# Thresholded attention with a gated mix: the first batch's softmax division moved behind the attended values, and a third PSUM room for scores at the start

## The chip, the cores and the metric

One NeuronCore of a Trainium2 chip runs the whole program. The metric is the device time of one execution in microseconds (us); a run's time is that of its slowest core, and here there is one. A profiled execution has its own time and, a little shorter, its span: from the first to the last instruction that the profile shows.

## The reference

There are 8 batches of 8 heads, 576 positions and a head size of 64. Attention keeps only the scores within `tau` of their row's maximum; the attended values of a batch's heads, side by side, are the input of a gated mix with 512 channels.

```python
scores = scale * np.matmul(q, k.transpose(0, 1, 3, 2))
thresh = np.max(scores, axis=-1, keepdims=True) - tau
scores = np.where(scores >= thresh, scores, -1000000000.0)
scores = scores - np.max(scores, axis=-1, keepdims=True)
attn = np.exp(scores)
attn = attn / (np.sum(attn, axis=-1, keepdims=True) + 1e-09)
x = np.matmul(attn, v)                     # heads side by side: (batch, 576, 512)
...
for k in range(K):                         # K = 5
    gate_pre += conv_w[k][None, None, :] * xp[:, k:k + S, :]
gate = 1.0 / (1.0 + np.exp(-gate_pre))
val = x @ w_val
return (gate * val @ w_out).astype(np.float32)
```

## The kernel before

A **job** is two heads of one batch: 32 jobs, four for each batch. A job has two **halves** of the query positions (320 and 256 columns, `W`), and its scores come in nine **tiles** of 128 rows by 576 keys: four query blocks for each of the two heads, and one tile that holds the last 64 positions of both heads ("both"). A **group** is what is turned together: the two heads' tiles of one query block, side by side in a `pp` buffer, or the "both" tile in the `pl` buffer.

A tile passes through these steps (class `Tile`):

- `multiply` (L493, TensorE): the scores, into one of two PSUM rooms `s` of two banks each (`r_s`).
- `largest` (L497, VectorE): the row maximum, negated, into `nm`.
- `weigh` (L503 and L505, ScalarE): the exponential into `e`, and the threshold into `nm`.
- `keep` (L519, VectorE): scores over the threshold keep their weight, into `pp` or `pl`, and a column of `sums` takes the row sum. With it the room `s` becomes free.

Then the group's softmax division (`Group.turned`): 1e-9 is added on GpSimd (L536), VectorE makes the reciprocal (L538), and each tile's 576 columns are multiplied by it on GpSimd (L549) or ScalarE (L545), whichever the planner finds free. TensorE turns the divided weights in three steps of three 128x128 transposes (L599; the "both" tile: four and one) into one of two one-bank rooms `tp`, and ScalarE copies each step into `T` (L610, L615, L621). When a half's `T` is full, `attended` multiplies it with the values (L643) into a one-bank room `acc` and ScalarE copies that to `xT` (L651). These matmuls come in pairs, one for each head, and the two heads fill different halves of the array's columns. The first pair takes the last 64 keys and stands there as three pieces:

```python
pieces = [(0, NKC, 0, SL), (1, NKC, 0, w), (0, NKC, SL, w)]
```

The mix needs `xT`: in the first batch its five taps are float32 matmuls with diagonal matrices (L690, GpSimd makes the diagonals at L677), in the other batches they run on GpSimd and VectorE (L730, L737). The two 512x512 products (L784) of a batch fill gaps of TensorE while the next batches' tiles are worked on. Job 0's scores are float32 matmuls of the raw inputs; from job 1 on they are made of two parts each (`KH`, `KL`, `Q`), which ScalarE (L331, L340) and GpSimd (L292) split and SyncE's DMA queue lays out. In the first batch VectorE, ScalarE and GpSimd also unpack both weight matrices, in sixteen blocks (`Words`, `from_f64`).

The order of all instructions is written out by a planner in the kernel (`op`, `carry_out`): every operation has an engine, a cost, a due time, what it comes after, and the rooms it takes and gives. The planner walks through its own time and emits, on each engine, the ready operation that is due first. Engines then work off their instructions strictly in that order. PSUM has eight banks: four are the rooms `s`, two `tp`, two `acc`.

Of the kernel before, what the change touches and what calls it, by code (L numbers as in the profile page):

```python
# [10 lines left out]
F32 = mybir.dt.float32  # L11
# [7 lines left out]
P = 128  # L19
# [2 lines left out]
DIVIDE = ("ACT",)  # L22
DUE = (8, 8, 8)
PACE_M = 0.17
ON_PE = (0, 1, 2, 3)


@with_exitstack
def tile_thresholded_attention_gated_mix(
# [42 lines left out]
    ps_a = ctx.enter_context(tc.tile_pool(name="ps_a", bufs=1, space=bass.MemoryType.PSUM))  # L72

    ctx.enter_context(tc.manual_schedule())

# [119 lines left out]
    r_pp = Rooms(att, 3, [P, 2 * S], F32, "pp")  # L195
    r_pl = Rooms(att, 1, [P, S + SL], F32, "pl")
    r_sums = Rooms(att, 5, [P, 4], F32, "sums")
    r_T = Rooms(pt, 2, [P, 2 * NKC + 1, W[0]], F32, "T")
    r_xT = Rooms(mix, 2, [P, PAD + S], F32, "xT")
    r_xh = Rooms(mix, 6, [P, S], F32R, "xh")  # L200
# [231 lines left out]
            self.lent = lambda: room.rearrange("p (e s) -> p e s", e=NE)  # L432


    class Tile:
        def __init__(self, k, t, h, qc, grp):
            self.k, self.t, self.h, self.qc, self.grp = k, t, h, qc, grp
            i = h or 0
            both = h is None
            if both:  # L440
                after = t.blocks if t.i == 0 else [t.high_k, t.low_k, *t.blocks]
            elif t.i == 0:
                after = [t.first[h]]
            else:
                after = t.copied
            if tiles:
                after = after + [tiles[-1].scores]
# [12 lines left out]
            if TH == "ACT":  # L460
                after = [op("ACT", k - DUE[1], 0.83, 1.0, self.weigh, [largest], [r_e])]
            else:
                after = [
                    op("ACT", k - DUE[1], 0.64, 0.78, self.weigh, [largest], [r_e]),
                    op("DVE", k - 9, 0.13, 0.13, self.level, [largest]),
                ]
            room = [] if i else [r_pl if both else r_pp]
            if i:
                after.append(grp.kept)
            grp.kept = op(  # L470
                "DVE", k - DUE[2], 0.74, 0.96, self.keep, after, room + ([] if i else [r_sums]),
                [(r_s, lambda: self.s), (r_e, lambda: self.e), (r_nm, lambda: self.nm)],
            )

        def multiply(self):
            t, h, qc = self.t, self.h, self.qc
# [37 lines left out]
        def keep(self):  # L514
            grp, i = self.grp, self.h or 0
            if i == 0:
                grp.p = (r_pl if grp.both else r_pp).take()
                grp.sums = r_sums.take()
            nc.vector.scalar_tensor_tensor(  # L519
                grp.p[:, i * S : (i + 1) * S].rearrange("p (a f) -> p a f", a=2),  # L520
                self.s[:, :, :HS], self.nm[:, 1:2], self.e,
                op0=ALU.is_ge, op1=ALU.mult, accum_out=grp.sums[:, i : i + 1],
            )

    class Group:


        def __init__(self, half, off, both):
            self.half, self.off, self.both = half, off, both

        def turned(self, k):

            n = 1 if self.both else 2
            sums = lambda: self.sums[:, 0:n]
# [25 lines left out]
            if self.both:  # L560
                divided.append(op("POOL", k - 4, 0.21, 0.3, lambda: spread(
                    self.p[:, S : S + SL], self.p[:, S - SL : S]), divided))
            parts = [(0, NKC), (NKC, 1)] if self.both else [(0, 3), (3, 3), (6, 3)]
            out = []
            for c0, m in parts:
                last = c0 + m == (NKC + 1 if self.both else 2 * NKC + 1)
                half = self.half
                turn = op(
                    "PE", k - 3 + 0.1 * c0, 0.109 * m, 0.109 * (m - 1) + 0.35, self.turn(c0, m),
                    divided if last else divided[0 : 1 + c0 // 3 * (n - 1)], [r_tp],  # L570
                    [(r_pl if self.both else r_pp, lambda: self.p)] if last else [],
                )
# [53 lines left out]
    class Half:  # L626
        def __init__(self, t, j):
            self.t, self.j = t, j
            self.T, self.begun, self.room, self.copies = None, False, [], []

        def attended(self, k):
            t, j = self.t, self.j
# [2 lines left out]
            def attend():  # L635
                acc = self.acc = r_acc.take()
                T = self.T[:, :, 0:w]
                pieces = [(0, NKC, 0, SL), (1, NKC, 0, w), (0, NKC, SL, w)]
                pieces += [(h, c, 0, w) for c in range(NKC) for h in range(2)]
                for n, (h, c, q0, q1) in enumerate(pieces):  # L640
                    c0 = (2 * c + h) * D
                    chunk = 2 * NKC if c == NKC else h * NKC + c
                    nc.tensor.matmul(  # L643
                        acc[HEADS[h], q0:q1], t.v[:, c0 : c0 + D], T[:, chunk, q0:q1],
                        start=n < 2, stop=c == NKC - 1, skip_group_check=True,
                    )
# [13 lines left out]
            t.got_x = op("ACT", k - 4, cost, cost + 0.2, evacuate, after, [r_xT] if j == 0 else [],  # L660
                         [(r_acc, lambda: self.acc)])
            t.got_half.append(t.got_x)


# [204 lines left out]
        conv_w.bitcast(I32).rearrange("(c p) k -> p c k", p=P),  # L869
    )  # L870
    make_identity(nc, ident)
    for _, t in r_bd.free:
        nc.gpsimd.memset(t.bitcast(F32), 0.0)
    for _, t in r_xT.free:
# [84 lines left out]
```

## Time and profile before

| | |
|---|---|
| time, median of 3 runs | 757.72 us (755.23 to 758.7) |
| profiled execution: its time, its span | 756.97 us, 755.2 us |
| TensorE (PE) busy | 728.2 us, 96% of the span |
| VectorE (DVE) busy | 601.5 us, 80% |
| ScalarE (ACT) busy | 639.4 us, 85% |
| GpSimd (POOL) busy | 539.7 us, 71% |

"Busy" is the share of time in which an engine had an instruction in work. On TensorE it hides short stalls, since matmuls overlap: one of 288 columns is shown with some 0.29 us while the next begins 0.13 us after it. PEld is the load of a matmul's fixed operand. PEclk is the granted TensorE clock as a share of 2.4 GHz; 0.5 is 1.2 GHz.

### The profile page before, as it was taken

Reading aid. Unit: us, or ns where it says so; the run is one execution under the profiler, and the core shown is the slowest. Engines: PE = TensorE matmul, PEld = TensorE weight load, DVE = VectorE, ACT = ScalarE, POOL = GpSimd, SP = SyncE. Lnnn points to the kernel's source line nnn. Section 1 sums busy time; section 2 is a strip of 40 time slices with the busy share of each in tenths; the row PEclk is TensorE's granted clock in tenths of the full one; section 3 lists DMA queues with packets and bytes.
Section 4 is the critical chain, followed back from the end, with each engine's and each line's share of the span. In section 5 each row is a group of like instructions: output and inputs, shape, how many; then the busy total and the mean of one; then the engine's idle time right before and its main releaser. Section 6 shows DMA issues by size and latency. Waiting matters only on the chain.

```text
span 755.2 us, 16467 instructions
## 1 busy us (share of the span) xinstructions
PE 728.2 (96%) x5550; PEld 624.9 (83%) x5550; DVE 601.5 (80%) x1290; ACT 639.4 (85%) x1470; POOL 539.7 (71%) x892
## 2 busy tenths in 40 slices
PE   4999999999999999999999999999999999999997
PEld 3577778888889888898888888988888778888897
DVE  4588888999789988888788888888878778888630
ACT  3698999999998989998898999989988879888832
POOL 3778877876787886788677866887677876765431
PEclk9899999999999999999999999999999999999999
DMA  5465664645662665546555446545564455540001
GB/s 167 101 169 161 177 161 113 170 123 133 160 171 62 159 171 142 132 119 153 153 151 127 115 131 166 130 126 142 128 159 111 120 152 138 138 103 25 32 33 62
DMA packets 51283, 97.96 MB, mean 130 GB/s; under 512 B 8960, under 2 KB 8960, under 8 KB 51200
## 3 DMA queue, kind: packets, MB, share of 16 engines
q1 hardware_dynamic: 51040, 96.61, 49.5%
q8 instruction: 44, 0.72, 0.4%
q10 hardware_dynamic: 160, 0.31, 0.2%
q14 instruction: 39, 0.32, 0.1%
HBM read 34.62 MB, written 9.44 MB: 58 GB/s over the span
## 4 chain that ended last, share of the span: by engine, by line
PE 84%; DVE 5%; ACT 4%; POOL 3%; DMA 1%; issue 1%; SPq 0%; POOLq 0%; ACTq 0%
PE acc L784 24%; PE acc L643 21%; PE s L493 21%; PE tp L599 17%; DVE nm L497 2%; PE acc L690 2%; DVE pp L519 2%; ACT e L503 1%; ACT T L610 1%; DMA q_r<-qT 1%; POOL gl L292 1%; DMA pre<-kT 1%; POOL pp L549 1%; DVE pre L737 0%; ACT xh L720 0%
## 5 line engine op out<-in xcount | busy, mean ns | idle before, releaser
L497 DVE TENSOR_REDUCE nm<-s 128x1 f32<-128x576 f32 x288 | 216.0, 754 | 59.7 <-PE s L493 56.2
L503 ACT ACTIVATE e<-s,nm 128x576 f32<-128x576 f32 x288 | 215.1, 747 | 29.8 <-DVE nm L497 16.0
L519 DVE SCALAR_TENSOR_TENSOR pp<-s,nm,e 128x576 f32<-128x576 f32 x256 | 207.7, 813 | 35.0 <-ACT nm L505 32.2
L610 ACT COPY T<-tp 128x384 f32<-128x384 f32 x384 | 175.1, 486 | 21.6 <-PE tp L599 20.5
L599 PE MATMUL tp<-ident,pp 128*128 128x128 f32 x1152 | 178.9, 275 | 3.3 <-POOL kl L292 1.8
L643 PE MATMUL acc<-T,v 128*64 128x256 f32 (+3 forms) x1408 | 172.4, 393 | 0.3 <-ACT T L610 0.2
L549 POOL TENSOR_SCALAR pp<-pp,sums 128x576 f32<-128x576 f32 x172 | 142.6, 834 | 40.4 <-DVE sums L538 30.2
L493 PE MATMUL s<-KH,Q 128*128 128x288 f32 x496 | 154.1, 326 | 4.2 <-DVE pp L519 3.8
L599 PEld LDWEIGHTS tp<-ident,pp 128*128 128x128 f32 x1152 | 139.1, 141 | 10.5 <-ACT T L610 2.6
L643 PEld LDWEIGHTS acc<-T,v 128*64 128x64 f32 x1408 | 97.1, 138 | 54.4 <-issue 10.7
L493 PE MATMUL s<-KL,Q 128*128 128x288 f32 x496 | 138.7, 295 | 0.0
L493 PEld LDWEIGHTS s<-KH,Q 128*128 128x128 f32 x496 | 94.4, 190 | 25.9 <-DVE pp L519 9.0
L737 DVE SCALAR_TENSOR_TENSOR pre<-xT,cw,pre 128x576 f32<-128x576 f32 x112 | 106.6, 952 | 10.2 <-POOL pre L730 10.0
L493 PEld LDWEIGHTS s<-KL,Q 128*128 128x128 f32 x496 | 93.9, 189 | 0.2
L536 POOL TENSOR_SCALAR sums<-sums 128x2 f32<-128x2 f32 (+1 forms) x160 | 45.6, 285 | 58.2 <-DVE pp L519 36.4
L505 ACT ACTIVATE nm<-nm,less 128x1 f32<-128x1 f32 x288 | 84.6, 294 | 0.0
L784 PE MATMUL acc<-gl,woh 128*128 128x320 f32 (+1 forms) x256 | 79.1, 309 | 2.6 <-POOL gl L292 2.6
L784 PE MATMUL acc<-gh,woh 128*128 128x320 f32 (+1 forms) x256 | 79.0, 309 | 0.0
L784 PE MATMUL acc<-xh,wvh 128*128 128x320 f32 (+1 forms) x256 | 78.8, 308 | 0.0
L784 PE MATMUL acc<-gh,wol 128*128 128x320 f32 (+1 forms) x256 | 78.3, 306 | 0.0
L784 PE MATMUL acc<-xl,wvh 128*128 128x320 f32 (+1 forms) x256 | 78.3, 306 | 0.0
L784 PE MATMUL acc<-xh,wvl 128*128 128x320 f32 (+1 forms) x256 | 77.8, 304 | 0.0
(85 smaller groups left out, 1253.5 us busy)
## 6 DMA issues: line engine op xcount, KB each, us to landing
KH<-kh SPq DMA_DIRECT2D x124, 144.0 KB, 2.5
KL<-kl SPq DMA_DIRECT2D x124, 144.0 KB, 3.5
v<-vs SPq DMA_DIRECT2D x32, 320.0 KB, 3.1
k_r<-kT SPq DMA_DIRECT2D x31, 320.0 KB, 3.9
outT<-o SPq DMA_DIRECT2D x32, 288.0 KB, 2.3
q_r<-qT SPq DMA_DIRECT2D x31, 288.0 KB, 3.6
Q<-qh SPq DMA_DIRECT2D x62, 128.0 KB, 2.2
Q<-ql SPq DMA_DIRECT2D x62, 128.0 KB, 2.4
```

The lines of the kernel that those rows point to most:

```text
L493: nc.tensor.matmul(s[:, a, :HS], w, m, start=i == 0, stop=i == len(terms) - 1)
L497: nc.vector.tensor_reduce(self.nm[:, 0:1], self.s[:, :, :HS], axis=AX.XY, op=ALU.max, negate=True)
L503: nc.scalar.activation(self.e, self.s[:, :, :HS], AF.Exp, bias=self.nm[:, 0:1])
L505: nc.scalar.activation(self.nm[:, 1:2], self.nm[:, 0:1], AF.Identity, bias=less, scale=-1.0)
L519: nc.vector.scalar_tensor_tensor(grp.p[:, i * S : (i + 1) * S].rearrange("p (a f) -> p a f", a=2), self.s[:, :, :HS], self.nm[:, 1:2], self.e,
L536: add = op("POOL", k - 4, 0.2, 0.33, lambda: nc.gpsimd.tensor_scalar(sums(), sums(), 1.0, 1e-9, op0=ALU.mult, op1=ALU.add), [self.kept])
L549: nc.gpsimd.tensor_scalar(v, v, ri(i), 0.0, op0=ALU.mult, op1=ALU.add)
L599: nc.tensor.transpose(tp[:, i * P : (i + 1) * P], self.p[:, k0 : k0 + P], ident)
L610: nc.scalar.copy(T[:, c0 : c0 + n, self.off : self.off + P], tp[:, 0 : n * P].rearrange("p (c q) -> p c q", q=P),)
L643: nc.tensor.matmul(acc[HEADS[h], q0:q1], t.v[:, c0 : c0 + D], T[:, chunk, q0:q1], start=n < 2, stop=c == NKC - 1, skip_group_check=True,)
L737: nc.vector.scalar_tensor_tensor(cv, t.xT[:, i : i + S], cw[:, g, i : i + 1], cv, op0=ALU.mult, op1=ALU.add)
L784: nc.tensor.matmul(taken[name, e, j][:, :w], wt[:, c, c0 : c0 + P], moving(c, i)[:, hs], start=n == 0, stop=n == NM - 1,)
```

## The change

For jobs of batch 0 (`LATE = 1`) the groups of two heads are no longer divided. `keep` writes the four tiles' row sums of a half into one tile `all`; the transposes take the undivided weights as soon as `keep` has written them. A new step of the half, `inverses`, adds 1e-9 to the four sums (GpSimd), makes four reciprocals (VectorE), spreads them to 128x256 (`wide`, GpSimd), turns that with two transposes (TensorE) into a room `tp`, and copies it to `R` (ScalarE). `evacuate` then writes `xT` as `acc` times `R`, on VectorE, where it was a copy on ScalarE. The "both" tile is still divided as before; the 64 columns of `R` that stand for it are set to one at the start. Other batches are divided as before.

The pool of `acc` is no longer opened at the start. Its two banks are first a third score room, `s2`, until the first tile with number 3 or more (`EARLY`) gives that room back; then its pool is closed and that of `acc` opened. By the written order two tiles use the room, the third and the sixth.

In all batches `attend` issues the first pair as two whole matmuls, so that a half has 10 of them where it had 11.

```diff
+EARLY = 3
+LATE = 1
...
-    r_acc = Rooms(ps_a, 2, [P, 512], F32, "acc")
+    r_acc = Rooms(None, 0, None, None, None)
+    ps_x = tc.tile_pool(name="ps_x", bufs=1, space=bass.MemoryType.PSUM)
+    third = ps_x.__enter__().tile([P, 2, 512], F32, name="s2")
+    r_s.free.append((0.0, third))
...
+    r_all = Rooms(att, 2, [P, 8], F32, "all")
+    r_wide = Rooms(att, 1, [P, W[1]], F32, "wide")
+    r_R = Rooms(att, 2, [P, W[0]], F32, "R")
...
+    class Scores:
+        def give(self, room, when):
+            if room is third and self.k >= EARLY:
+                ps_x.__exit__(None, None, None)
+                ps_a = ctx.enter_context(tc.tile_pool(name="ps_a", bufs=1, space=bass.MemoryType.PSUM))
+                r_acc.free = [(when, ps_a.tile([P, 512], F32, name=f"acc{i}")) for i in range(2)]
+            else:
+                r_s.give(room, when)
...
+            self.after = half.t.b < LATE and not both
...
+            divided = self.keeps if self.after else self.divided(k)
...
+        def inverses(self, k):
+            n = NKC
+            add = op("POOL", k - 3, 0.2, 0.33, lambda: nc.gpsimd.tensor_scalar(
+                self.sums[:, 0:n], self.sums[:, 0:n], 1.0, 1e-9, op0=ALU.mult, op1=ALU.add),
+                self.kept)
+            inv = op("DVE", k - 3, 0.08, 0.33, lambda: nc.vector.reciprocal(
+                self.sums[:, n : 2 * n], self.sums[:, 0:n]), [add])
...
+            wide = op("POOL", k - 2.7, 0.34, 0.45, widen, [inv], [r_wide], [(r_all, lambda: self.sums)])
+            turned = op("PE", k - 2.5, 0.218, 0.46, turn, [wide], [r_tp], [(r_wide, lambda: self.wide)])
+            return op("ACT", k - 2.5, 0.27, 0.44, copy, [turned], [r_R], [(r_tp, lambda: self.rp)])
...
-                pieces = [(0, NKC, 0, SL), (1, NKC, 0, w), (0, NKC, SL, w)]
-                pieces += [(h, c, 0, w) for c in range(NKC) for h in range(2)]
...
+                for c in (NKC, *range(NKC)):
+                    for h, hs in enumerate(HEADS):
...
-                nc.scalar.copy(t.xT[:, x0 : x0 + w], self.acc[:, :w])
+                if t.b < LATE:
+                    nc.vector.tensor_mul(t.xT[:, x0 : x0 + w], self.acc[:, :w], self.R[:, W[0] - w :])
+                else:
+                    nc.scalar.copy(t.xT[:, x0 : x0 + w], self.acc[:, :w])
```

The planner puts the steps in another order from the first tile on, and since its own time runs differently from there, all five queues differ in places up to the last job; the last 200 or so matmuls are the same.

TensorE at the start, before (`s0`, `s1` are score rooms, `tp` the transposes' rooms, `acc` the attended values):

```order
L493 MATMUL s0_101<-pre0_154 128x288 x2
L493 MATMUL s1_102<-pre0_154 128x288 x2
L493 MATMUL s0_101<-pre0_154 128x288 x2
L493 MATMUL s1_102<-pre0_154 128x288 x2
L599 MATMUL tp0_103<-ident_96,pp0_129 128x128 x3
L493 MATMUL s0_101<-pre0_154 128x288 x2
L599 MATMUL tp1_104<-ident_96,pp0_129 128x128 x3
...
L493 MATMUL s0_101<-pre0_154 128x288 x2
L643 MATMUL acc0_105<-T0_138,v0_113 64x64
L643 MATMUL acc0_105<-T0_138,v0_113 64x320
L643 MATMUL acc0_105<-T0_138,v0_113 64x256
L643 MATMUL acc0_105<-T0_138,v0_113 64x320 x8
L493 MATMUL s1_102<-kh0_109,bdq0_121 128x288 x2
```

and now, the same stretch and the first half's end:

```order
L520 MATMUL s0_98<-pre0_158 128x288 x2
L520 MATMUL s1_99<-pre0_158 128x288 x2
L520 MATMUL s2_105<-pre0_158 128x288 x2
L520 MATMUL s0_98<-pre0_158 128x288 x2
L640 MATMUL tp0_100<-ident_93,pp0_128 128x128 x3
L520 MATMUL s1_99<-pre0_158 128x288 x2
L640 MATMUL tp1_101<-ident_93,pp0_128 128x128 x3
...
L693 MATMUL tp0_100<-ident_93,wide0_139 128x128 x2
L640 MATMUL tp1_101<-ident_93,pl0_131 128x128 x4
...
L520 MATMUL s1_99<-kh0_108,bdq0_120 128x288 x2
...
L714 MATMUL acc0_290<-T0_142,v0_112 64x320 x10
```

Three tiles' scores stand before the first wait for a room where there were two, the two transposes of `wide` are new, and the first attend stands behind job 1's first tile (`kh`, `bdq`) where it stood ahead of it.

VectorE at the start, before:

```order
L497 TENSOR_REDUCE nm1_126<-s1_102 128x1
L519 SCALAR_TENSOR_TENSOR pp0_129,sums0_133<-s0_101,nm0_125,e0_123 128x576
L519 SCALAR_TENSOR_TENSOR pp0_129,sums0_133<-s1_102,nm1_126,e1_124 128x576
L229 TENSOR_SCALAR cw1_173<-cw_raw_171 128x20
L231 SCALAR_TENSOR_TENSOR cw0_172<-cw_raw_171,cw1_173 128x20
L497 TENSOR_REDUCE nm2_127<-s0_101 128x1
```

and now, with the first evacuation of `acc` further down:

```order
L524 TENSOR_REDUCE nm1_125<-s1_99 128x1
L551 SCALAR_TENSOR_TENSOR pp0_128,all0_137<-s0_98,nm0_124,e0_122 128x576
L524 TENSOR_REDUCE nm2_126<-s2_105 128x1
L551 SCALAR_TENSOR_TENSOR pp0_128,all0_137<-s1_99,nm1_125,e1_123 128x576
L524 TENSOR_REDUCE nm3_127<-s0_98 128x1
...
L551 SCALAR_TENSOR_TENSOR pl0_131,sums1_133<-s1_99,nm1_125,e1_123 128x576
L723 TENSOR_TENSOR xT0_144<-acc0_290,R0_140 128x320
L679 RECIPROCAL all1_138<-all1_138 128x4
L524 TENSOR_REDUCE nm2_126<-s0_98 128x1
```

The third tile's maximum stands between the first two `keep`s, and the evacuation stands ahead of the next tile's maximum. By count of the written order TensorE has 64 matmuls fewer in the attended values and 16 transposes more; VectorE 8 multiplications more and 8 reciprocals fewer; ScalarE 10 divisions of `pp` fewer, 3 of `pl` more, 8 copies to `xT` fewer and 8 to `R` more; GpSimd 25 divisions and 16 additions to `sums` fewer, 8 additions to `all` and 8 spreads more. The number of DMAs is the same.

## Rows read from the trace of the kernel before

**Rows 1.** Windows by stage: us, busy PE, PEld, DVE, ACT, POOL (count), clock, DMA.

```profile
0.00:34.70 34.70, 22.43 (x77) 13.89 (x79) 17.43 (x44) 17.78 (x38) 18.96 (x53) 0.90 0.50 138
34.70:125.20 90.50, 85.23 (x591) 69.22 (x587) 76.97 (x185) 80.10 (x194) 71.60 (x124) 1.00 0.60 159
125.20:700.00 574.80, 569.99 (x4496) 495.56 (x4496) 487.44 (x1026) 516.02 (x1181) 431.52 (x694) 1.00 0.53 133
```

**Rows 2.** Timeline of PE, 6 to 32 us: start, length, what, [idle before <-releaser].

```profile
6.21 2.39 PE L493 MATMUL s<-pre 64*128 64x288 f32 x8 [6.21 <-DMA pre<-kT]
11.13 3.10 PE L493 MATMUL s<-pre 64*128 64x288 f32 x8 [2.53 <-DVE pp L519]
16.04 0.87 PE L599 MATMUL tp<-ident,pp 128*128 128x128 f32 x3 [1.81 <-POOL kl L292]
16.71 2.13 PE L493 MATMUL s<-pre 128*128 128x288 f32 x4
18.63 1.49 PE L599 MATMUL tp<-ident,pp 128*128 128x128 f32 x6
20.05 1.70 PE L493 MATMUL s<-pre 64*128 64x288 f32 x4
...
23.33 1.23 PE L493 MATMUL s<-pre 64*128 64x288 f32 x4 [0.72 <-DVE pl L519]
...
28.19 2.28 PE L493 MATMUL s<-pre 64*128 64x288 f32 x4
```

**Rows 3.** Timelines of DVE, ACT and POOL, the first tiles.

```profile
8.50 1.42 DVE L497 TENSOR_REDUCE nm<-s 128x1 f32<-128x576 f32 x2 [2.59 <-PE s L493]
10.25 0.82 DVE L519 SCALAR_TENSOR_TENSOR pp<-s,nm,e 128x576 f32<-128x576 f32 x1 [0.33 <-ACT nm L505]
13.46 0.76 DVE L497 TENSOR_REDUCE nm<-s 128x1 f32<-128x576 f32 x1 [1.26 <-PE s L493]
...
15.14 0.76 ACT L545 ACTIVATE pp<-pp,sums 128x576 f32<-128x576 f32 x1
...
5.46 0.88 POOL L215 TENSOR_SCALAR pre<-pre 64x64 f32<-64x64 f32 x2 [3.43 <-DVE pre L424]
```

**Rows 4.** Timeline of PE: the first attend, job 1's first tile, and a later attend.

```profile
30.40 5.00 PE L643 MATMUL acc<-T,v 128*64 128x64 f32 x22
35.34 0.53 PE L493 MATMUL s<-kh,bdq 128*128 128x288 f32 x2
...
125.17 2.92 PE L643 MATMUL acc<-T,v 128*64 128x64 f32 x22
```

**Rows 5.** Windows of 0 to 45 us, columns as in rows 1.

```profile
21.02:27.85 6.83, 5.11 (x25) 2.95 (x24) 4.73 (x11) 5.98 (x14) 5.45 (x19) 1.00 0.64 172
27.85:34.67 6.82, 6.82 (x23) 3.53 (x25) 3.89 (x9) 3.06 (x8) 5.71 (x14) 0.50 0.00 0
```

**Rows 6.** Waits, 34 to 126 us: total us, times, longest.

```profile
DVE pp L519 <- ACT nm L505: 4.8, 13, 0.8
PE s L493 <- DVE pp L519: 3.4, 3, 1.4
ACT xT L651 <- PE acc L643: 3.2, 5, 1.5
```

**Rows 7.** Groups by line: 34.7 to 125.2 us, and the whole span: busy us, mean ns.

```profile
L545 ACT ACTIVATE pp<-pp,sums 128x576 f32<-128x576 f32 x9 | 7.0, 776 | 0.9 <-DVE sums L538 0.9
...
L811 DVE SCALAR_TENSOR_TENSOR g<-pre,acc 128x320 f32<-128x320 f32 x32 | 15.4, 483 | 4.5 <-PE acc L784 4.5
```

**Rows 8.** Windows of one attend, L643 on PE alone: its first pair, then whole pairs.

```profile
125.17:125.76 0.60, 0.60 (x6) 1.00 0.63 151
125.76:126.30 0.54, 0.54 (x6) 1.00 0.12 23
```

**Rows 9.** Groups by form on PE, at 125.17 us and from 125.75 to 126.8 us.

```profile
L643 PE MATMUL acc<-T,v 128*64 128x320 f32 x1 | 0.5, 482 | 0.0
L643 PE MATMUL acc<-T,v 128*64 128x320 f32 x9 | 1.5, 432 | 0.0
```

More of the change, by code (lines that the diff above doesn't have):

```diff
@@ L469, in __init__ @@
                 after.append(grp.kept)
+            elif grp.after:
+                after += grp.half.kept[-1:]
+                room += [] if grp.half.kept else [r_all]
+            else:
+                room.append(r_sums)
             grp.kept = op(
-                "DVE", k - DUE[2], 0.74, 0.96, self.keep, after, room + ([] if i else [r_sums]),
-                [(r_s, lambda: self.s), (r_e, lambda: self.e), (r_nm, lambda: self.nm)],
-            )
+                "DVE", k - DUE[2], 0.74, 0.96, self.keep, after, room,
+                [(Scores(k), lambda: self.s), (r_e, lambda: self.e), (r_nm, lambda: self.nm)],
+            )
+            grp.keeps.append(grp.kept)
+            if grp.after:
+                grp.half.kept.append(grp.kept)
         def multiply(self):
@@ L517, in keep @@
                 grp.p = (r_pl if grp.both else r_pp).take()
-                grp.sums = r_sums.take()
+                if not grp.after:
+                    grp.sums, grp.c0 = r_sums.take(), 0
+                else:
+                    if grp.half.sums is None:
+                        grp.half.sums = r_all.take()
+                    grp.sums = grp.half.sums
             nc.vector.scalar_tensor_tensor(
@@ L529, in __init__, with divided @@
             self.half, self.off, self.both = half, off, both
-        def turned(self, k):
+            self.after = half.t.b < LATE and not both
+            self.c0 = 2 * ((off - (SL if half.j == 0 else 0)) // P)
+            self.keeps = []
+        def divided(self, k):
             n = 1 if self.both else 2
@@ L562, in turned @@
                     self.p[:, S : S + SL], self.p[:, S - SL : S]), divided))
+            return divided
+        def turned(self, k):
+            n = 1 if self.both else 2
+            divided = self.keeps if self.after else self.divided(k)
             parts = [(0, NKC), (NKC, 1)] if self.both else [(0, 3), (3, 3), (6, 3)]
@@ L569, in turned @@
                     "PE", k - 3 + 0.1 * c0, 0.109 * m, 0.109 * (m - 1) + 0.35, self.turn(c0, m),
[L570 removed]
+                    divided if last else divided[0 : 1 + min(1, c0 // 3) * (n - 1)], [r_tp],
                     [(r_pl if self.both else r_pp, lambda: self.p)] if last else [],
@@ L629, in __init__, with widen, turn, copy @@
             self.T, self.begun, self.room, self.copies = None, False, [], []
+            self.sums, self.kept = None, []
+        def inverses(self, k):
[5 more added lines that the diff above has]
+                self.sums[:, n : 2 * n], self.sums[:, 0:n]), [add])
+            def widen():
+                self.wide = r_wide.take()
+                spread(
+                    self.wide.rearrange("p (c d) -> p c d", c=n),
+                    self.sums[:, n : 2 * n].unsqueeze(2).to_broadcast([P, n, D]),
+                )
+            def turn():
+                self.rp = r_tp.take()
+                for i in range(n // 2):
+                    cols = slice(i * P, (i + 1) * P)
+                    nc.tensor.transpose(self.rp[:, cols], self.wide[:, cols], ident)
+            def copy():
+                self.R = r_R.take()
+                nc.scalar.copy(self.R[:, SL:], self.rp[:, 0 : W[1]])
+            wide = op("POOL", k - 2.7, 0.34, 0.45, widen, [inv], [r_wide], [(r_all, lambda: self.sums)])
+            turned = op("PE", k - 2.5, 0.218, 0.46, turn, [wide], [r_tp], [(r_wide, lambda: self.wide)])
+            return op("ACT", k - 2.5, 0.27, 0.44, copy, [turned], [r_R], [(r_tp, lambda: self.rp)])
         def attended(self, k):
@@ L637, in attend @@
                 T = self.T[:, :, 0:w]
-                pieces = [(0, NKC, 0, SL), (1, NKC, 0, w), (0, NKC, SL, w)]
-                pieces += [(h, c, 0, w) for c in range(NKC) for h in range(2)]
[L640 to L646, printed above, removed]
+                for c in (NKC, *range(NKC)):
+                    for h, hs in enumerate(HEADS):
+                        c0 = (2 * c + h) * D
+                        chunk = 2 * NKC if c == NKC else h * NKC + c
+                        nc.tensor.matmul(
+                            acc[hs, :w], t.v[:, c0 : c0 + D], T[:, chunk, :],
+                            start=c == NKC, stop=c == NKC - 1, skip_group_check=True,
+                        )
             def evacuate():
@@ L659, in attended @@
             after = [made] if j == 0 else [made, t.got_x]
-            t.got_x = op("ACT", k - 4, cost, cost + 0.2, evacuate, after, [r_xT] if j == 0 else [],
-                         [(r_acc, lambda: self.acc)])
+            gives = [(r_acc, lambda: self.acc)]
+            if t.b < LATE:
+                cost += 0.085
+                after.append(self.inverses(k))
+                gives.append((r_R, lambda: self.R))
+            t.got_x = op("DVE" if t.b < LATE else "ACT", k - 4, cost, cost + 0.2, evacuate, after,
+                         [r_xT] if j == 0 else [], gives)
             t.got_half.append(t.got_x)
@@ L871, in tile_thresholded_attention_gated_mix @@
     make_identity(nc, ident)
+    for _, t in r_R.free:
+        nc.gpsimd.memset(t[:, 0:SL], 1.0)
     for _, t in r_bd.free:
```

6 lines of the change are left out of this document (4 added, 2 removed).

## The prediction

> **What bounds the kernel now.** I read the windows by stage first. From 125 to 700 us TensorE is busy for 569.99 of 574.80 us [rows 1]: there it is the bound, and only fewer matmuls or fewer stalls shorten the time. In the first batch, 34.7 to 125.2 us, it is busy for 85.23 of 90.50 us, with ScalarE at 80.10 and VectorE at 76.97: 5.27 us of TensorE idle, against the 0.84% (0.76 us) that the later stage would leave in as long a stretch. So some 4.5 us are to be had there. In the first 34.7 us it is busy for 22.43 only, and part of that is at the lower clock. That is where the timeline comes in [rows 2, 3]: the first tiles run as a relay. Two score tiles are made by 8.5 us; the third must wait until VectorE's first `keep`, begun at 10.25, has freed a room, so that TensorE stands idle to 11.13. The first transposes, at 16.04, stand behind a division that ScalarE begins at 15.14 (the profile puts that wait down to GpSimd's `kl`, the last to signal; the division ends at 15.90). The sixth, seventh and ninth tiles start at 20.05, 23.33 and 28.19 [rows 2], and the first attend at 30.40 [rows 4].
>
> **The start, step by step.** I walk the new order with the durations of these rows. One raw tile takes half of 2.39 us, some 1.0 at the lower clock [rows 2]. A maximum takes 0.7, a `keep` 0.82; the first maximum ends near 9.2 and its `keep` begins at 10.25, so that some 1.0 us of ScalarE lies between [rows 3]. Three transposes take 0.67 (16.04 to 16.71), the "both" tile 1.9 (16.71 to 18.63) [rows 2].
> - The third tile follows the second on TensorE and is there at 9.5. Its maximum stands behind the first `keep`: 11.07 to 11.74, where it began at 13.46 [rows 3].
> - The second `keep` then ends at 12.56 and the third at 14.05. The fourth tile's scores start at 11.13 as before the third's did.
> - The first transposes need no division: 12.1 in place of 16.04. The "both" tile starts at 12.7 in place of 16.71.
> - The sixth, seventh and eighth tiles start at 15.9, 17.5 and 19.8; the ninth waits for a `keep` that ends at 22.5, and starts there in place of 28.19.
> - The "both" tile's weights are still divided, on GpSimd, near 21 us; its transposes come at 21.3 and hold the rest by about half a microsecond.
> - The attend starts at 24.4 in place of 30.40, with job 1's first tile (35.34 to 36.24, 0.9 us [rows 4]) and three more transposes at the full clock (0.33) already done.
>
> The lead is 30.40 − 24.4 + 0.9 + 0.33, less the two new transposes that I count below: **7.0 us**. It is a chain on VectorE, ScalarE and TensorE, with waits in it; no other term hides it, and it carries to the end since TensorE does the same work behind it. Its ends: 2.4 us, the one stall that the room ends for certain (13.46 to 11.07), and 8.
>
> **The clock.** From 27.85 to 34.67 us the granted clock was 0.50 (1.2 GHz) and it was 1.00 after that [rows 5]; before it fell, from 21.02, TensorE was busy for 5.11 of 6.83 us and stood idle between the tiles. The first attend ran in that stretch and took 5.00 us, a later one 2.92 [rows 4]: 2.1 us. In the walk above TensorE has some 0.6 us more to do from 21 to 27.85, and most of it is attend in place of transposes. I take it that the clock stays up, and **2.1 us** are gained. The other end: it falls all the same from 27.85 on, now with TensorE busy throughout, and 6.82 us at half speed cost 3.4. TensorE: Matmul & The Clock Gate of the Trainium skill, Part 1, has the throttled clock as the default that activity releases: by it the fuller stretch keeps the clock, as in my sum. But its Part 4 says that a transpose does not count as busy in the same way, and that speaks against this change, which brings transposes forward; by that the 2.1 would become a loss of 3.4. Rows 5 cannot separate the two.
>
> **The rest of the first batch.** The 32 divisions of `pp` are gone there. ScalarE had 9 of them, 7.0 us [rows 7], from its 80.10; the copies to `R` and those no longer made to `xT` are 8 each and cancel. GpSimd loses the others, which is worth nothing by itself: it had 18.9 us free. VectorE gains 8 multiplications from PSUM. The trace has no such operation; the nearest, L811, reads `acc` and a second tensor and takes 483 ns at 320 columns [rows 7], so 0.4 to 0.48 each, some 3.5 us on an engine with 13.5 free. The 8 reciprocals saved are under 0.1 each; I count none. What TensorE waits for there is `keep` (3.4 us), which waits for ScalarE's threshold (4.8 us) [rows 6]: less work on ScalarE shortens the second and so the first. But the multiplication now stands in VectorE's queue ahead of the next maximum and waits for the attend; ScalarE's copy waited 3.2 us in 5 cases [rows 6]. Of the 4.5 us I take a third: **1.5 us**; ends 0 and 4.5.
>
> **Transposes added.** 16 of 0.11 us (half of 0.67 / 3, since the clock is twice as high): **1.8 us** on the bounding engine, charged in full. Should they fall into stalls they cost nothing. The spreads on GpSimd and the additions stand ahead of them in time by over a microsecond, since the half's attend waits for the same last `keep` and its copies. The two memsets of `R` lie in the 3.43 us that GpSimd waits for VectorE at the start [rows 3]. DMAs are as many as before; the loads and layouts of job 1 come in a slightly other order, and their cover is the attend and three tiles ahead of the first matmul that uses them.
>
> **One matmul fewer in each half.** The first pair of an attend, in three pieces, took 0.60 us, a whole pair 0.54 [rows 8]: 64 halves of 0.06 would be 3.8 us on the bound. But the first matmul of an attend is longer by itself: 482 ns for the 320 columns that are not split, against 432 for later ones [rows 9]. That 0.05 stays when the split goes. I take 0.01 a half, **0.7 us**, by these rows; ends 0 and 3.8. The Trainium skill's VectorE: DVE Perf Modes, section on the TRN2 errata, gives a matmul 6 cycles beside its columns; by that the split costs some 0.3 us in all, and the trace agrees so far as 0.05 of the 0.06 us lie in the first matmul.
>
> **The sum**, against the profiled execution's own 756.97 us: −7.0 − 2.1 − 1.5 + 1.8 − 0.7 = −9.5, so 747.5. The median of the runs stands 0.75 above that execution, so **748.2 us**. The later batches' order is shuffled too; the stalls there are 4.8 us in all [rows 1], so I allow 2.5 either way and count none.
>
> **The rivals.**
> - **The clock falls all the same** (or stays down longer). For it: it fell before after a stretch in which TensorE was busy for 75% [rows 5]. Against it: the stretch is fuller now. 748.2 + 2.1 + 3.4 is 753.7; with a part of the half-speed stretch 751 to 753. Chance 0.2.
> - **The lead is eaten up in the first batch.** Job 1's and job 2's parts and the weights are made by ScalarE, VectorE and GpSimd, and a lead of TensorE's chain counts only if these come earlier too. For it: VectorE and ScalarE are busy for 85% and 89% there. Against it: ScalarE and GpSimd lose work. Then 748.2 + 7.0: 755.2, no change that can be measured. Chance 0.13.
> - **VectorE is held by the attends.** Each of the 8 multiplications waits at the head of VectorE's queue until its attend has ended; behind it stand the maxima and `keep`s that free the score rooms, and TensorE soon waits for those. If VectorE gets there as the attend begins, it loses the attend's 2.92 us (some 2.3 for the smaller halves) and the 0.64 that ScalarE's copy waited on average: 26.0 us in all. VectorE has some 10 free in the stage. The rest, 16.0, and the 1.5 not won give 765.7: slower. It decides from 1.2 us of wait for each multiplication on. Against it: the planner orders these by its own estimate of the attend's end. Chance 0.04.
> - **The room does nothing**, because VectorE alone paces the first tiles. Against it: VectorE stood idle for 2.59 and 1.26 us before two of the first maxima [rows 3]. It would leave about half the lead, by the division's removal: 751.7. Chance 0.08.
>
> **How the numbers follow.** The forecast has 0.55, the rivals 0.45. Half a per cent, 3.8 us, is what a measurement here can tell from no change: faster is below 753.9, slower above 761.5. Faster: the forecast, the fourth rival, three quarters of the first and a third of the second: 0.82. Same: the rest of the first two: 0.14. Slower: the third, 0.04. The range: down to 740 (the whole stage's stalls won, 3.0, the split's full price, 3.1, and a part of the shuffle's 2.5), up to 755 (the clock's fall with 1.3 of shuffle on top, and half of the second rival). Left out are some 2 in 10.
>
> **What would show it.** After the change the third maximum on VectorE begins near 11.1 us, the first transposes near 12, the first attend near 24.5. The clock is 1.00 in all windows after 21 us. TensorE's idle in the first batch falls from 5.3 to under 4 us. An attend takes 2.83 us, not 2.78. VectorE waits less than 1 us before each multiplication. The prediction is wrong if the first attend starts after 27 us, if VectorE's waits for the attends add up to more than 10 us, or if the stalls after 125 us grow by more than 2.5.

## The result and the profile after

The changed kernel takes **750.66 us** (median of 6 runs, 747.82 to 752.66), the kernel before 757.13 (6 runs, 755.23 to 759.74): a ratio of 0.9917, 95% interval 0.9891 to 0.9942. It is faster by 6.5 us; 8.9 were forecast on the medians, and the time lies 2.5 us above the 748.2 forecast, inside the range. The profiled execution took 752.66 us (span 750.7), the highest of its six, so the two profiled executions differ by 4.3 us only. The account below is of these two.

The changed kernel's windows by stage, in the columns of [rows 1]:

```profile
0.00:34.70 34.70, 27.32 (x121) 18.61 (x121) 20.93 (x52) 20.06 (x47) 16.37 (x46) 1.00 0.57 152
34.70:125.20 90.50, 83.60 (x571) 64.88 (x570) 80.14 (x186) 75.40 (x187) 62.63 (x116) 1.00 0.62 161
125.20:700.00 574.80, 569.07 (x4407) 491.37 (x4407) 482.42 (x1024) 516.20 (x1186) 424.98 (x691) 1.00 0.52 132
```

Against [rows 1], TensorE is busy for 4.9 us more of the first 34.7 us. In the first batch it is idle for 6.90 us, where it was 5.27 and under 4 was forecast. The next view is the timeline of PE in the changed kernel, the counterpart of [rows 2, 4]: start, length, what, idle before.

```profile
6.06 4.17 PE L520 MATMUL s<-pre 64*128 64x288 f32 x12 [6.06 <-DMA pre<-kT]
10.98 2.29 PE L520 MATMUL s<-pre 64*128 64x288 f32 x4 [0.75 <-DVE pp L551]
13.20 0.90 PE L640 MATMUL tp<-ident,pp 128*128 128x128 f32 x3
13.89 2.13 PE L520 MATMUL s<-pre 128*128 128x288 f32 x4
...
17.23 1.79 PE L520 MATMUL s<-pre 64*128 64x288 f32 x4
...
19.43 1.24 PE L520 MATMUL s<-pre 64*128 64x288 f32 x4
...
24.22 1.23 PE L520 MATMUL s<-pre 64*128 64x288 f32 x4 [0.22 <-DVE pp L551]
...
26.76 2.91 PE L714 MATMUL acc<-T,v 128*64 128x320 f32 x20
29.61 0.88 PE L640 MATMUL tp<-ident,pp 128*128 128x128 f32 x6
...
120.41 2.91 PE L714 MATMUL acc<-T,v 128*64 128x320 f32 x20
```

Three tiles are made without a stop, the wait of 2.53 us for VectorE's `keep` has shrunk to 0.75 one tile later, and the first transposes start at 13.20 instead of 16.04. The sixth to the ninth tile start 2.8 to 4.0 us earlier than in [rows 2]; the first attend starts at 26.76 instead of 30.40.

TensorE's waits in the changed kernel, 34 to 126 us, as in [rows 6]: total us, times, longest.

```profile
PE s L520 <- DVE pp L551: 2.8, 4, 1.0
PE tp L640 <- ACT T L651: 2.1, 3, 0.9
PE tp L640 <- ACT R L697: 1.5, 3, 0.9
```

The last row is new: the two transposes of `wide` take one of the two `tp` rooms, and the next turn of weights waits until ScalarE has copied `R` out of it.

**An account of the whole span.** I split TensorE's time in three: idle time, work, and what the lower clock adds to the work. The last is half of what TensorE was busy at 1.2 GHz, in windows cut where the granted clock changes. First the changed kernel (the clock's record begins at 18.39, at full speed, and the view prints 1.00 for the window ahead of it too; that the clock was at the lower level there is seen in the raw tile of 2.29 us at 10.98, against 1.24 at 19.43):

```profile
0.00:18.39 18.39, 11.58 (x32) 7.96 (x33) 8.15 (x19) 7.85 (x17) 5.02 (x19) 1.00 0.52 152
18.39:34.67 16.28, 15.70 (x91) 10.65 (x89) 12.75 (x33) 12.18 (x30) 11.33 (x27) 1.00 0.63 152
...
125.20:560.00 434.80, 429.07 (x3316) 369.33 (x3315) 364.23 (x773) 389.57 (x897) 326.30 (x531) 1.00 0.54 138
560.00:750.70 190.70, 186.03 (x1437) 163.98 (x1435) 134.86 (x280) 148.19 (x338) 112.83 (x179) 1.00 0.36 96
```

and the same of the kernel before (its record begins at 21.02; the two windows behind it are [rows 5]):

```profile
0.00:21.02 21.02, 10.47 (x31) 7.42 (x32) 8.78 (x24) 8.74 (x18) 7.77 (x22) 1.00 0.62 171
...
125.20:560.00 434.80, 433.11 (x3427) 377.64 (x3428) 372.82 (x784) 393.63 (x904) 331.51 (x535) 1.00 0.55 139
560.00:755.20 195.20, 187.43 (x1464) 164.14 (x1460) 134.24 (x280) 147.89 (x336) 117.63 (x181) 1.00 0.36 94
```

The changed kernel's lower clock costs 11.58 / 2 = 5.8 us. The one before has 10.47 and, from [rows 5], 6.82 at the lower level: 8.65. Idle is each window less its busy time. For these two and for four experiments told below, in us:

| kernel (profiled execution) | span | work at full clock | lower clock | idle to 125.2 | idle 125.2 to 560 | idle from 560 |
|---|---|---|---|---|---|---|
| before | 755.2 | 719.6 | 8.7 | 17.5 | 1.7 | 7.8 |
| changed | 750.7 | 720.2 | 5.8 | 14.3 | 5.7 | 4.7 |
| split_only | 753.0 | 718.9 | 5.4 | 19.9 | 2.5 | 6.3 |
| room_only | 751.8 | 719.3 | 10.2 | 13.0 | 4.1 | 5.2 |
| late_only | 755.8 | 720.4 | 12.6 | 13.7 | 2.0 | 7.1 |
| pieces_back | 748.1 | 720.8 | 4.2 | 13.9 | 4.5 | 4.7 |

So the change won 2.9 us of clock and 3.2 of idle time up to 125 us; it pays 0.7 in work; of the later idle time it loses 4.0 and wins 3.1. Each row stands for one execution, and halving is an estimate.

### The profile page after: what moved, and what is told of

Read it like the earlier page. It is cut to its first block, busy times and chain, and to the rows that moved or that the text cites. A ratio compares the mean times of both kernels' runs of the same rounds, so it can differ in the third digit from the quotient of the medians.

```text
span 750.7 us, 16257 instructions
## 1 busy us (share of the span) xinstructions
PE 726.0 (97%) x5438; PEld 616.8 (82%) x5438; DVE 600.2 (80%) x1290; ACT 633.2 (84%) x1463; POOL 518.1 (69%) x869
## 4 chain that ended last, share of the span: by engine, by line
PE 77%; POOL 6%; ACT 5%; DVE 5%; DMA 3%; issue 2%; SPq 1%; POOLq 0%; ACTq 0%; DVEq 0%
PE acc L863 23%; PE s L520 19%; PE acc L714 18%; PE tp L640 16%; DMA q_r<-qT 2%; DVE pp L551 2%; ACT e L530 2%; POOL pp L584 1%; ACT T L651 1%; PE acc L769 1%; DVE nm L524 1%; POOL kl L299 1%; DMA Q<-ql 1%; POOL gl L299 1%; POOL q_r L355 1%
## 5 line engine op out<-in xcount | busy, mean ns | idle before, releaser
L714 PE MATMUL acc<-T,v 128*64 128x256 f32 (+1 forms) x1280 | 169.3, 411 | 1.4 <-ACT T L651 1.3
L584 POOL TENSOR_SCALAR pp<-pp,sums 128x576 f32<-128x576 f32 x150 | 122.6, 823 | 26.8 <-DVE sums L573 19.6
L714 PEld LDWEIGHTS acc<-T,v 128*64 128x64 f32 x1280 | 86.2, 136 | 63.0 <-issue 5.3
L816 DVE SCALAR_TENSOR_TENSOR pre<-xT,cw,pre 128x576 f32<-128x576 f32 x112 | 102.8, 918 | 11.6 <-POOL pre L809 11.4
L571 POOL TENSOR_SCALAR sums<-sums 128x2 f32<-128x2 f32 (+1 forms) x144 | 39.1, 271 | 64.9 <-DVE pp L551 51.0
```

The lines of the kernel that those rows point to most:

```text
L571: add = op("POOL", k - 4, 0.2, 0.33, lambda: nc.gpsimd.tensor_scalar(sums(), sums(), 1.0, 1e-9, op0=ALU.mult, op1=ALU.add), [self.kept])
L584: nc.gpsimd.tensor_scalar(v, v, ri(i), 0.0, op0=ALU.mult, op1=ALU.add)
L714: nc.tensor.matmul(acc[hs, :w], t.v[:, c0 : c0 + D], T[:, chunk, :], start=c == NKC, stop=c == NKC - 1, skip_group_check=True,)
L816: nc.vector.scalar_tensor_tensor(cv, t.xT[:, i : i + S], cw[:, g, i : i + 1], cv, op0=ALU.mult, op1=ALU.add)
```

## The experiments

**The parts one by one.** Four kernels ran beside the same runs of the kernel before (756.7 us, 29 runs).

`split_only` is the kernel before with whole first pairs in `attend`:

```
-                pieces = [(0, NKC, 0, SL), (1, NKC, 0, w), (0, NKC, SL, w)]
...
+                for c in (NKC, *range(NKC)):
+                    for h, hs in enumerate(HEADS):
```

> The kernel before with the first pair of every attend issued as two whole matmuls, all else and the whole order as before. My term: 0.01 us a half, 0.7 us in all, so a ratio to before of 0.999 (756.4 of 757.13 us), and an attend of 320 columns that lasts 2.84 us from its first matmul to the next instruction where it lasted 2.85. Rival: the split itself cost 0.06 us a half: 3.8 us, ratio 0.995, attends of 2.78 us.

Measured: 755.65 us (12 runs), ratio 0.9985 (0.9965 to 1.0004). The price by itself is seen in the trace: from its first matmul to the next instruction an attend of 320 columns takes a median of 2.846 us before and 2.843 with whole pairs, one of 256 columns 2.313 and 2.310. That is 0.003 us a half, 0.2 us in all. (The column of work has 0.7 and 0.6 us between kernels that differ by the split alone, so it is good to about half a microsecond.) The profiled executions differ by 2.2 us of span, and by the account that is something else: 3.3 us of clock, which rose at 21.25 us and stayed up, against 2.4 us more of idle time up to 125 us.

`pieces_back` is the changed kernel with the old three pieces, the opposite edit.

> The changed kernel with the three pieces of the first pair put back; order otherwise that of the changed kernel. By my term it is 0.7 us slower than the changed kernel (751.4 of 750.66), by the rival 3.8 us (754.5).

Measured: 751.68 us (6 runs), ratio 0.9914 (0.9892 to 0.9936), the same as the change's 0.9917. The split carries no part of the gain. The account shows what makes its profiled execution the faster one by 2.6 us of span: 1.6 us of clock, which rose at 15.37 us instead of 18.39, and 1.2 us less of idle time behind 125 us.

`room_only` is the kernel before with the third score room alone:

```
-    r_acc = Rooms(ps_a, 2, [P, 512], F32, "acc")
+    r_acc = Rooms(None, 0, None, None, None)
+    ps_x = tc.tile_pool(name="ps_x", bufs=1, space=bass.MemoryType.PSUM)
+    third = ps_x.__enter__().tile([P, 2, 512], F32, name="s2")
+    r_s.free.append((0.0, third))
...
-                [(r_s, lambda: self.s), (r_e, lambda: self.e), (r_nm, lambda: self.nm)],
+                [(Scores(k), lambda: self.s), (r_e, lambda: self.e), (r_nm, lambda: self.nm)],
```

> The kernel before with the third score room alone: division as before. My theory: the room ends the wait of the third tile (its maximum begins near 11 us in place of 13.5), but the transposes still stand behind the division, so the first attend begins 2 to 3 us earlier than before (30.40), near 28; the clock may fall as before. Time 752 to 756 us. Rival, VectorE alone paces the first tiles: the attend begins within 0.7 us of 30.40 and the time is that of before. Second rival, the room makes nearly the whole lead: attend near 26.8, as in the changed kernel.

Measured: 755.6 us (12 runs, 749.86 to 757.24), ratio 0.9975 (0.9956 to 0.9994). Its windows, cut at the changes of the clock:

```profile
0.00:9.89 9.89, 3.60 (x12) 2.90 (x12) 2.61 (x7) 2.00 (x3) 2.22 (x13) 1.00 0.74 226
9.89:13.31 3.42, 2.19 (x9) 1.20 (x8) 3.09 (x8) 2.71 (x8) 0.94 (x2) 1.00 0.16 63
13.31:30.37 17.06, 16.86 (x50) 11.01 (x49) 10.01 (x29) 11.20 (x25) 10.33 (x23) 0.50 0.54 136
```

From 13.31 us TensorE has hardly a gap, but it works at the lower level until 30.37: 16.86 us that would be 8.4. The third tile's maximum begins at 11.08 us, as expected, but the first attend at 32.36, later than before, and later than the theory or either rival had it. These windows stand for one run: its mean granted clock is 0.988, while the other eleven have 0.999 to 1.0, ten of them with 754.99 to 757.24 us and one with 749.86. That mean covers only the part of a run for which there is a record, and the record can begin late, as it does in the next kernel; a mean of 1.0 does not show that the start ran at full speed.

`late_only` is the change without the third room: the division behind the attends, `wide`, `R` and the multiplication, with the old pieces.

> The changed kernel with two score rooms from the start (and the three pieces): the division of the first batch moved, no third room. My theory: the first transposes come at about 12.5 us in place of 16.04, the third tile's maximum stays at 13.5, and the first attend begins near 28; the clock stays up, since the attend is nearer. Time 750 to 754 us. Rival, the division makes the whole lead: attend near 26.8 and the changed kernel's time (751.4 with the pieces). Second rival, the first batch gets nothing from it: the time is that of before, 755 or more.

Measured: 757.56 us (12 runs), ratio 0.9997 (0.9983 to 1.0012): nothing, where 750 to 754 was expected; the second rival has the time. The first transposes start at 14.01 us (12.5 expected), the first attend at 32.53 (28). Its first window:

```profile
0.00:34.68 34.68, 25.22 (x71) 15.30 (x73) 17.46 (x43) 16.22 (x38) 18.41 (x53) 1.00 0.55 145
```

The record of the clock begins only at 34.68 us. TensorE is busy for 25.22 us here, 2.8 more than in [rows 1]. A raw tile takes 2.29 us as late as 30.31, so I take all of it to be at the lower level: the account has 12.6 us for it.

What follows: the room alone brings −0.25% and the division alone −0.03%; both together, with the old pieces, −0.86%, three times the sum. In the account each of room and division wins some 4 us of idle time up to 125 us, and gives 1.6 and 3.9 of it back to the clock. Together they win 3.2 of idle time, less than either alone, and the clock comes up earlier than before. So my theory became: what joins the parts is the clock. The rival was that they need one another in the order of the work, whatever the clock.

**The clock held up from the start.** Eleven matmuls on zeros were put ahead of the first score tile, from 1.5 us on, while TensorE waits for the first load; they write a `tp` room before anything of use is in it. `w_hl` is allocated earlier for that, and WARM is 11. The edit, in each of four kernels:

```
+    w_hl = {
+        name: [const.tile([P, NE, DM], F32R, name=name + p) for p in "hl"] for name in ("wv", "wo")
+    }
+    still = w_hl["wv"][0][:, 0, :]
+    nc.vector.memset(still.bitcast(F32), 0.0)
...
+    for _ in range(WARM):
+        nc.tensor.matmul(r_tp.free[0][1], still[:, 0:P], still, start=True, stop=True)
```

> The kernel before with 11 matmuls of a zeroed 128x512 tile on TensorE while the first inputs load, so that its clock is up when job 0's scores begin, if it stays up through the gaps. Clock theory (what the two parts of the change do together is to let the clock rise at 15 to 18 us, where it rose near 21 before and near 32 in the two halves of the change): 2 to 5 us faster than before, 752 to 755 us, with the first attend 2 to 3 us earlier. Relay theory (the chain over VectorE and ScalarE alone sets the start): within 1.5 us of before. Third possibility: the clock falls again in the gaps of job 0, and nothing is gained.

> The third room alone, with the same 11 matmuls ahead. Clock theory: its late rise (30 us in its profile) goes, 4 to 6 us faster than the room alone (755.6), 750 to 752. Relay theory: within 1.5 us of 755.6.

> The moved division alone, with the same 11 matmuls ahead. Clock theory: its late rise (34.7 us in its profile) goes, 4 to 7 us faster than that part alone (757.56), 751 to 753. Relay theory: within 1.5 us of 757.56.

> The changed kernel with the same 11 matmuls ahead. Clock theory: it had the clock up from 15 to 18 us, so only the first tiles gain: 1 to 3 us, 748 to 750. Relay theory: as the changed kernel, 750.7. If it is below 749 it beats both kernels.

Measured, as ratios to the kernel before (756.69 us, 29 runs): `warm_before` 753.96 us, 0.9963 (0.9946 to 0.9979); `warm_room` 751.67, 0.9940 (0.9914 to 0.9965); `warm_late` 756.52, 0.9997 (0.9983 to 1.0011); `warm_after` **746.40**, 0.9859 (0.9833 to 0.9884). Against the clock theory's bands the times of `warm_before` and `warm_room` came out as expected, `warm_late` missed (751 to 753) and lies where the relay theory has it, and `warm_after` is faster than 748 to 750. In `warm_before` the time follows the mean clock: 752.89 to 753.77 us in the five runs at 0.995, 758.45 at 0.983, the profiled one, in which the clock was at the lower level from 11.05 to 34.94 us. The changed kernel gains 4.3 us more by the zeros. Its windows show the clock up from 5.59 us on:

```profile
0.00:5.59 5.59, 4.11 (x10) 3.24 (x11) 1.52 (x6) 1.49 (x2) 1.78 (x14) 1.00 0.55 136
5.59:34.67 29.08, 25.15 (x141) 17.29 (x139) 24.00 (x57) 21.27 (x52) 18.68 (x41) 1.00 0.71 190
```

Its first attend starts at 22.38 us. In `warm_late` the clock rises and then falls again, in the old gap ahead of the third tile (2.65 us, up to 10.36):

```profile
0.00:9.80 9.80, 6.22 (x19) 4.18 (x19) 3.53 (x9) 2.76 (x5) 2.39 (x15) 1.00 0.74 219
9.80:37.10 27.30, 25.86 (x75) 14.91 (x75) 15.07 (x37) 13.91 (x34) 16.92 (x40) 0.50 0.49 127
```

`warm_room` makes the price plain: its twelve runs are of two kinds by their mean granted clock. Six with a clock of 1.0 took 748.62 to 750.36 us, six with 0.986 to 0.989 took 752.98 to 756.88. The program is the same; some 5 us hang on whether the clock stays up in the first 31 us.

**The gaps filled too.** To keep the clock up where it had fallen, more such matmuls were put into the gaps ahead of the third to fifth tiles, in `multiply`:

```
+            for _ in range(FILL.get(self.k, 0)):
+                nc.tensor.matmul(r_tp.free[0][1], still[:, 0:P], still, start=True, stop=True)
```

> The kernel before, with 11 matmuls on zeros ahead of the first tile, 12 ahead of the third and 4 ahead of the fourth, so that TensorE has no gap there. If the clock decides: it stays at 1.00 in the first 35 us and the time is 752 to 753.5, near the faster runs of the version with zeros at the start alone (753.0). If the zeros only delay the tiles, the time is 755 or more with the clock at 1.00.

> The kernel before with the third room, and zeros at the start (11), ahead of the fourth tile (8) and the fifth (4). If the clock decides: 1.00 in the first 35 us and 748.5 to 750.5 in all runs, as in the six faster runs of the version with zeros at the start alone. If the two kinds of run there had another cause than the clock, they stay two kinds, with 753 to 757 among them.

> The change without the third room, and zeros at the start (11), ahead of the third tile (12) and the fourth (4). If the division's removal was worth nothing alone (757.56) because the clock stayed down to 34.68 us: the clock is 1.00 here from about 6 us on, the first attend starts near 25, and the time is 749 to 752. If the division needs the third room for itself, whatever the clock: 753 to 757, as much as the kernel before with zeros or more.

> The changed kernel with zeros at the start (11) and ahead of the fourth tile (8). The clock was at 1.00 there with the first zeros alone (746.4), so the clock theory expects no change: 746 to 747. If the gap of 1.69 us still cost clock in some runs, up to 1 us less.

Measured, beside 19 runs of the kernel before (755.89 us): `fill_before` 753.68 us (10 runs), 0.9974 (0.9960 to 0.9988); `fill_room` 751.17 (4 runs, 749.88 to 751.72, all at a clock of 1.00), 0.9929 (0.9903 to 0.9954); `fill_late` 753.36 (10 runs), 0.9960 (0.9943 to 0.9977); `fill_after` 746.20 (4 runs), 0.9867 (0.9843 to 0.9891).

`fill_before` is 0.2 us above its band, and its clock did not stay up either: in its profile it is at the lower level from 26.88 to 30.29 us. The room came out as the clock theory has it: one kind of run, 4.4 us below `room_only`, though 0.7 above the expected band. The changed kernel stayed where it was, since its clock was up already. **The division alone missed**: 749 to 752 was expected, and 753.36 lies in the rival's band, only 0.3 us below `fill_before`. Two things stand in its trace. First, the clock did not stay up after all:

```profile
7.28:27.76 20.48, 16.32 (x75) 10.33 (x72) 15.01 (x35) 12.64 (x31) 14.21 (x35) 1.00 0.63 175
27.76:31.18 3.42, 3.42 (x15) 1.77 (x15) 2.06 (x3) 2.15 (x5) 2.07 (x3) 0.50 0.37 81
```

By half of 3.42 that cost 1.7 us here. Three of the ten runs, this one among them, have a mean clock of 0.998 and took 752.06 to 752.39 us; the other seven have 0.995 and took 753.05 to 754.42, so most lost more to the clock than this trace shows.

Second, TensorE waits for GpSimd ahead of the last tile. Timeline of PE in `fill_late`:

```profile
24.20 0.38 PE L684 MATMUL tp<-ident,wide 128*128 128x128 f32 x2
26.91 0.33 PE L631 MATMUL tp<-ident,pl 128*128 128x128 f32 x1 [2.33 <-POOL pl L223]
27.17 1.74 PE L511 MATMUL s<-pre 64*128 64x288 f32 x4
28.84 4.05 PE L706 MATMUL acc<-T,v 128*64 128x64 f32 x22
```

and of POOL in the same kernel:

```profile
22.74 3.91 POOL L748 TENSOR_SCALAR pre<-ident,cw 128x128 f32<-128x128 f32 x10
26.62 0.24 POOL L223 TENSOR_SCALAR pl<-pl 128x64 f32<-128x64 f32 x1
```

The spread of `pl`, on which the last transposes wait, stands in GpSimd's queue behind ten diagonals of the taps, 3.91 us, that nothing needs yet. In the changed kernel VectorE makes the taps' weights later, and the spread is free of them (POOL, changed kernel):

```profile
23.85 0.24 POOL L222 TENSOR_SCALAR pl<-pl 128x64 f32<-128x64 f32 x1
...
27.24 1.56 POOL L756 TENSOR_SCALAR g<-ident,cw 128x128 f32<-128x128 f32 x4
```

And the first attends of `fill_before` and `fill_after`, with zeros in both:

```profile
26.49 4.61 PE L649 MATMUL acc<-T,v 128*64 128x64 f32 x22
```

```profile
22.37 2.91 PE L720 MATMUL acc<-T,v 128*64 128x320 f32 x20
```

So both theories have a part. With zeros in both, the change still gains 7.5 us (753.68 to 746.20), and its first attend starts 4.1 us earlier: the gain is an earlier start, and the clock makes little of it (the fall in `fill_before` costs by the same halving 1.7 us). The clock is worth some 4 us to the room and to the whole change, against 2.0 to the kernel before (ratio 0.9974), and it is why the room alone gives so little without zeros. For the division that is not shown: zeros take 0.37% off it and 0.26% off the kernel before.

The rival has the other part. With zeros in all four, the parts (−0.45% and −0.14% against `fill_before`'s ratio) still add up to less than the whole (−1.07%), a little over half of it. For the division the planner's order of GpSimd's work may be one reason, 2.33 us in the trace, of which `fill_before` has 1.19 too, behind the same diagonals. The clock's second fall can be another only as far as it is longer than that of `fill_before`. How the rest divides stays open: no kernel was run that moves the diagonals alone.

## Why the prediction came out as it did

- **The start's lead, −7.0: mis-sized.** At the first attend the measured lead is 5.0 us: 30.40 − 26.76 = 3.64, and 1.35 us of work at the full clock that now stands ahead of it (job 1's tile and five transposes, two of them `wide`'s; without these two, as the forecast counted, it is 4.8). The forecast called itself wrong from a first attend after 27 us on, so this came near. The wait named was the right one, and the start of the fourth tile was forecast to 0.15 us (11.13; 10.98). The step that failed is "a raw tile takes half of 2.39 us, some 1.0": the fourth tile took 2.29 alone. Two raw tiles, x8, take 2.39 us in [rows 2], and one, x4, takes 2.28 in the last of these rows: the two heads' tiles use 64 rows each and run beside one another, so half of the pair is no tile's time. The rows held the right number. With it the first transposes come at 13.2, as they did, instead of 12.1. The later raw tiles, each alone too, took 1.23 to 1.79; so the sixth tile was 1.3 us behind the walk (17.23; 15.9), the ninth 1.7, the attend 2.4. The third maximum, which hangs on VectorE alone, came at 10.84 (11.1 forecast).
- **The clock, −2.1: right in size, its reason not shown.** The clock stayed at 1.00 from 18.39 us on, where it fell at 27.85 before [rows 5]. The first attend took 2.91 us instead of 5.00, and behind it the lead has grown from 5.0 to 7.1 (35.34 − 29.61, and the same 1.35), against the 9.1 of the two terms together; by the account the lower level costs 2.9 us less in all. The reason given was that the stretch is fuller. In `room_only` a stretch as full did not bring the clock up; and in the kernel before the fall is not in every run: of the 77 runs beside the experiments, 7 have a mean clock as low as the 0.995 of its profiled execution. So there is luck in it that the clock came out as forecast. What I missed is that the clock also sets what each part is worth, and how much it differs from run to run. The first rival (it falls all the same) did not come in this kernel, though the parts alone behave like it.
- On the Trainium skill's TensorE: Matmul & The Clock Gate: the transposes were brought forward, to 13.20 to 17.3 us, and the clock rose behind them, so the loss that I worked out from its Part 4 did not come. Its Part 1 agrees with this trace, in which the clock rose once TensorE was at work, and does not tell why the clock of `room_only` stayed down from 13.31 to 30.37 us. Of the 16.86 us of work there 6.45 were transposes; no run took them out, so whether Part 4 bears on that stretch is open.
- **The rest of the first batch, −1.5: wrong in sign.** Idle time there grew from 5.27 to 6.90 us. "Less work on ScalarE shortens the second and so the first" failed: VectorE's `keep` still waits 5.2 us for ScalarE's threshold (4.8 in [rows 6]), TensorE's wait for `keep` fell by 0.6 only, and the waits for a `tp` room, of ScalarE's copies of `T` and of `R`, grew from 1.5 to 3.6 us. Of the lead of 7.1 us, 6.2 were left at the second attend and 5.25 at the end of the batch.
- **Transposes +1.8 and the split −0.7.** Work at the full clock grew by 0.7 us, against 1.1. The split is worth 0.2; "0.05 of the 0.06 us stay in the first matmul" was right, and nearly all of the rest stays too. The 0.3 worked out from VectorE: DVE Perf Modes of the Trainium skill was nearer. It was itself added up wrongly: six cycles for each of 64 halves are 0.16 us at 2.4 GHz, an estimate by that page, and nearer still.
- **The later order, ±2.5 and none counted: right in sum.** Idle time from 125.2 to 560 us grew by 4.0 us and fell by 3.1 behind that, 0.9 net; each alone is beyond the 2.5. In the last stage it was a wait for GpSimd's `gl` and one for `keep` (2.6 and 1.2 us before) of which 1.2 is left.
- **The rivals.** VectorE held by the attends (765.7) is refuted: the 8 multiplications take 414 ns at 256 columns and 492 at 320, and VectorE waited 0.3 us in all ahead of them. The room that does nothing is refuted by `late_only` and `pieces_back`, which differ by the room alone (757.56 and 751.68 us), and by `fill_room` against `fill_before`. The lead that is eaten up in the first batch came true for 1.8 us of 7.1.

In sum −9.5 was forecast on the profiled execution and −4.3 came, of which the mis-sized tile and the first batch's idle time make up most; on the medians −8.9 and −6.5. The 2.2 us between the two lie in which execution was profiled; its six runs spread over 4.8 us. So the median fits better than the terms do.

## What to carry to other kernels

Where the start of a kernel runs at the lower clock, price each edit there in idle time and in clock apart: an edit that closes gaps can give back in clock what it wins in idle time (1.6 and 3.9 of some 4 us here). A few matmuls on zeros under the first load brought the clock up and kept it up in the changed kernel (746.40 us, against 757.1 before and 750.7 for the change alone); in the profiled runs of the three others it fell again. Read a tile's duration from a row that holds that tile by itself, since two that run side by side cannot be halved. A part that measures as nothing alone may still be needed by the whole: test the parts in both directions, and look at what the planner moved into the place that the part freed. A mean clock of 1.0 says nothing of a stretch for which there is no record: time a tile there.

## What was not expected of the hardware

- Two raw tiles of 64 rows each take 1.25 us together at the full clock and 2.39 at the lower; one alone takes 1.23 and 2.28.
- The clock's rise is not bound to a place in the program: 21.02 and 21.25 us in two kernels with the same start, 15.37 and 18.39 in two others. In `room_only` it rose at 9.89, fell at 13.31 and came back at 30.37, though TensorE was busy for 16.86 of the 17.06 us between.
- One program, `warm_room`, gave medians of 749.5 and 755.3 us in two groups of six runs on one chip, and the mean granted clock told the two apart; in `room_only` it did not (749.86 to 757.24 us at 0.999 to 1.0).
